# Attention scores, a gate and a planned order: the gate score moved into the matmul of the reads, small work moved to GpSimd, new urgencies for the planner

## The chip, the cores and the metric

The kernel runs on one core of a Trainium2 chip. The metric is device time in microseconds, the median of three runs, and less is better. Five engines take part, each with a queue of its own that it works off in order: TensorE (PE in the profile, PEld for its weight loads), VectorE (DVE), ScalarE (ACT), GpSimd (POOL) and SyncE (SP, which here only issues DMAs). They wait for each other through semaphores.

## The reference

There are 8 batches. In each, 8 heads have 512 rows of x and 32 rows of state, 64 wide. The x rows read the state by softmax, and the state rows read x by softmax. Both results together, 544 rows of 512 (the heads side by side), are the input of a mixture-of-depths block: a gate score per row, the 128 rows with the highest scores of each batch go through two layers, and what comes out is added to them, times the sigmoid of the score.

```python
scores = scale * np.matmul(x, state.transpose(0, 1, 3, 2))
a = np.exp(scores - scores.max(-1, keepdims=True)); a /= a.sum(-1, keepdims=True) + 1e-09
xread = np.matmul(a, state)
...
sread = np.matmul(a2, x)
x = np.concatenate([xread, sread], axis=2)  # then (B, S, H*D)
scores = np.einsum('bsd,d->bs', x, w_gate)
top_idx = np.argpartition(-scores[b], capacity)[:capacity]
ye = np.maximum(x[b, top_idx] @ w1, 0.0) @ w2
out[b, top_idx] = x[b, top_idx] + g[:, None] * ye   # g is the sigmoid of the score
```

All data are float32; x is 8 x 8 x 512 x 64, w1 512 x 1024, w2 1024 x 512.

## The kernel before, in words

The program is cut into pieces (`add`), each a few instructions on one engine with a length in us, the pieces it comes after, the buffers it takes or uses, a key, and for a DMA the time until it has landed. `carry_out` plans all of them ahead of the run: it keeps a clock per engine, finds the engine on which a piece can start first, and among the pieces of that engine that can start within SOON (0.25 us) of it puts down the one with the lowest key. A piece on another engine is seen HOP (0.2 us) after its end. The order so found is the order of the instructions of each engine; on the chip it stays as it is, whatever the real times are. Buffers come from rings: a piece can take one only when all users of the buffer that held the place before it are planned.

One batch goes through these pieces. `attention`: four turns of x on TensorE into ps_tr (L302) with ScalarE copies to xT (L305); scores into ps_s (L325); on VectorE a 32 x 32 transpose into e (turn_in, L339), the maximum (L343), its subtraction (L346), exp on ScalarE (L349), sum and reciprocal (L353 to L355), the product (L358), a transpose into eT (turn_out, L361); for the state side a maximum (s_max, L367), exp on ScalarE (L371), the sums (L376, L377), two turns of a (L418) with copies (L421), the product with x (L434) and its scaling (L439). The reads of the state, `read` (L402), come in two pieces of 16 passes into the one buffer of ps_o, each followed by a ScalarE copy of 1024 columns to xs (L405). SP stores xs (L461) and the state rows (L466).

`choice`: the gate scores, four VectorE products of xs with wg that sum up (gate, L485), for the state rows a product (L491), a sum over heads on TensorE (L498) and a copy (L501). Then the scores are spread along rows (row_x L514, row_s L517, copies L520 and L523), compared with each other (win, L533), counted on TensorE (wins_over, L560) and turned to places (offsets L566, one_hot L573). parts (L544 to L547) splits the scores into three bf16 numbers. pick (L588) finds the chosen rows' numbers and scores, index (L592, L593) makes a row number of them. fetch is GpSimd's gather by row number out of the stored output (L473), which waits for the batch's stores. below (L602 to L604), exps (L607) and sigmoid (L611 to L613) make the gate's weight.

`layers`: it works on the rows of batch 0 alone, then 1 and 2, 3 and 4, 5 and 6, and 7 alone. The rows are turned (L644, copies to xg L647), go through the first layer (L661, relu L665) and the second (L678), VectorE adds (L681) and GpSimd writes the rows back by number (put, also L473). The keys: attention and choice of batch b have (b, n), the layers (100 + number, n), and relu, add and put (-1, number).

Setup: SP loads the first states (L167), x of batch 0 in four pieces (L246), the other states (L170), wg spread over 128 partitions (L174), x of 1 and 2, w1 (L256), x of 3, w2 (L259). GpSimd spreads the states into st_v (pool_states, L202 to L205 and L199) when both loads have landed, and then makes the tables (pool_tables, L211 to L224). row_numbers (L228 to L232) is on VectorE. The states are turned on TensorE (L276, L280). Buffers: ps_tr has two, ps_s and ps_o one of 1024 columns each, ps_h two, xf five (the first of them holds the states until they are spread and turned, and x of batch 4 takes its place).

## Time and profile before

| | us |
|---|---|
| device time, median of 3 runs | 248.92 |
| lowest and highest | 247.83, 250.1 |
| device time of the profiled execution | 248.68 |
| its span, first to last instruction | 246.9 |
| PE, DVE, ACT, POOL busy in it | 209.8, 145.8, 86.0, 32.4 |
| mean granted clock of TensorE | 0.92 of 2.4 GHz |

The profile is that of one execution. The span leaves out what lies ahead of the first instruction and behind the last, so the device time is a little longer. The granted clock of TensorE has two levels: 1.00 is 2.4 GHz, 0.50 is 1.2 GHz, and a number between is a stretch that holds both. A matmul of fp32 weights shows as two instructions.

### The profile page before, as it was taken

To read this page: it belongs to the slowest core of one execution; us is meant where nothing else is said; L and a number is where in the kernel's file an instruction comes from. 1 tells how busy PE (TensorE), PEld (TensorE's weight loads), DVE (VectorE), ACT (ScalarE), POOL (GpSimd) and SP (SyncE) were. 2 spreads that over 40 slices of the span, in tenths; PEclk is the share of its full clock that TensorE was granted. 3 is DMA by queue.
4 is the path that set the end of the run, shared out by engine and by line. 5 is a ranking of instruction groups with operands and counts; after the bars stand their busy time and mean duration, and the time that the engine had idled before them with its cause. 6 is when DMAs were issued, how large, how long until landed. Compare 5 with 4: busy or idle time off the path is not lost.

```text
span 246.9 us, 4781 instructions
## 1 busy us (share of the span) xinstructions
PE 209.8 (85%) x1928; PEld 150.7 (61%) x1928; DVE 145.8 (59%) x430; ACT 86.0 (35%) x159; POOL 32.4 (13%) x60
## 2 busy tenths in 40 slices
PE   2668837959999995774979999999999999999991
PEld 2457524748794663652867877656884478745940
DVE  0375999696899999889899998985000110011001
ACT  3366543644546553255535537111112001200000
POOL 5492000200100021020010001032000110001101
PEclk9977995786999999775999999999999999999998
DMA  6999392269445052050050030630200110001101
GB/s 178 281 379 323 71 357 96 85 234 322 135 136 226 0 190 83 11 212 0 24 206 1 23 150 11 216 98 21 66 0 3 42 42 1 0 0 45 42 0 42
DMA packets 17559, 26.86 MB, mean 109 GB/s; under 512 B 5632, under 2 KB 13824, under 8 KB 16512
## 3 DMA queue, kind: packets, MB, share of 16 engines
q1 hardware_dynamic: 16256, 22.35, 26.9%
q0 software_dynamic: 1280, 4.20, 5.1%
q8 instruction: 15, 0.25, 0.4%
q14 instruction: 8, 0.07, 0.1%
HBM read 15.53 MB, written 11.01 MB: 108 GB/s over the span
## 4 chain that ended last, share of the span: by engine, by line
PE 29%; DVE 28%; issue 28%; ACT 4%; DMA 4%; POOL 3%; SPq 2%; POOLq 1%; DVEq 0%; ACTq 0%
PE ps_o L402 7%; PE ps_h L678 6%; PE ps_h L661 4%; DVE scr L485 4%; DMA xf<-in_x_dram 4%; PE ps_tr L302 3%; DVE win L533 3%; DVE eT L361 3%; DVE e L358 2%; DVE sm L353 2%; DVE e L346 2%; DVE nm L367 2%; PE ps_tr L434 2%; PE ps_tr L418 2%; POOL out_dram L473 2%
## 5 line engine op out<-in xcount | busy, mean ns | idle before, releaser
L661 PE MATMUL ps_h<-xg,w 128*128 128x256 f32 (+1 forms) x320 | 59.5, 345 | 0.7 <-ACT xg L647 0.7
L678 PE MATMUL ps_h<-w,hT 128*128 128x512 f32 x128 | 58.0, 598 | 0.0
L661 PEld LDWEIGHTS ps_h<-xg,w 128*128 128x128 f32 x320 | 52.3, 196 | 7.3 <-issue 1.4
L681 DVE SCALAR_TENSOR_TENSOR ot<-ps_h,z,xr 128x512 f32<-128x512 f32 x8 | 6.0, 750 | 67.2 <-PE ps_h L678 67.2
L678 PEld LDWEIGHTS ps_h<-w,hT 128*128 128x128 f32 x128 | 23.3, 190 | 24.6 <-issue 24.3
L665 ACT ACTIVATE hT<-ps_h 128x512 f32<-128x512 f32 x16 | 9.5, 596 | 61.5 <-PE ps_h L661 61.5
L302 PE MATMUL ps_tr<-ident,xf 128*128 128x128 f32 x128 | 23.8, 344 | 5.6 <-DMA xf<-in_x_dram 4.5
L402 PE MATMUL ps_o<-st_v,eT 64*128 64x128 f32 x256 | 22.2, 323 | 4.6 <-DVE rs L376 4.2
L473 POOL DMA_INDIRECT xr<-out_dram,idx x8 | 8.9, 1112 | 125.2 <-DVE z L602 79.9
L305 ACT COPY xT<-ps_tr 128x512 f32<-128x512 f32 x32 | 18.2, 590 | 18.7 <-PE ps_tr L302 15.5
L405 ACT COPY xs<-ps_o 128x1024 f32<-128x1024 f32 x16 | 16.2, 1014 | 23.1 <-PE ps_o L402 23.1
L302 PEld LDWEIGHTS ps_tr<-ident,xf 128*128 128x128 f32 x128 | 18.3, 176 | 9.5 <-DMA xf<-in_x_dram 2.9
L402 PEld LDWEIGHTS ps_o<-st_v,eT 64*128 64x128 f32 x256 | 18.9, 223 | 7.8 <-DVE rs L376 5.4
L485 DVE SCALAR_TENSOR_TENSOR scr<-xs,wg 128x512 f32<-128x512 f32 x32 | 22.0, 686 | 2.2 <-ACT xs L405 1.3
L325 PE MATMUL ps_s<-xT,st_T 64*32 64x256 f32 x256 | 10.8, 447 | 9.6 <-ACT a L371 9.6
L473 POOL DMA_INDIRECT out_dram<-ot,idx x8 | 8.1, 1018 | 79.9 <-DVE ot L681 64.9
L533 DVE SCALAR_TENSOR_TENSOR win<-srow,sc,after 128x544 bf16<-128x544 f32 (+4 forms) x40 | 18.0, 508 | 0.7 <-ACT srow L523 0.7
L339 DVE STREAM_TRANSPOSE e<-ps_s 128x1024 f32<-128x1024 f32 x8 | 9.9, 1237 | 9.5 <-PE ps_s L325 9.5
L418 PE MATMUL ps_tr<-ident,a 128*128 128x128 f32 x64 | 11.0, 312 | 2.1 <-ACT xT L305 2.1
L325 PEld LDWEIGHTS ps_s<-xT,st_T 64*32 64x32 f32 x256 | 4.4, 120 | 13.7 <-ACT a L371 10.9
L421 ACT COPY aT<-ps_tr 128x512 f32<-128x512 f32 x16 | 9.1, 589 | 7.5 <-PE ps_tr L418 7.5
L349 ACT ACTIVATE e<-e 128x1024 f32<-128x1024 f32 x8 | 8.5, 1061 | 9.1 <-DVE e L346 9.1
(81 smaller groups left out, 221.1 us busy)
## 6 DMA issues: line engine op xcount, KB each, us to landing
out_dram<-xs SPq DMA_DIRECT2D x8, 1024.0 KB, 4.3
xf<-in_x_dram SPq DMA_DIRECT2D x14, 512.0 KB, 7.9
w<-in_moe_w_dram SPq DMA_DIRECT2D x2, 2048.0 KB, 12.8
xf<-in_x_dram SPq DMA_DIRECT2D x4, 256.0 KB, 4.3
out_dram<-xt SPq DMA_DIRECT2D x32, 16.0 KB, 1.8
xf<-in_state_dram SPq DMA_DIRECT2D x1, 448.0 KB, 5.7
wg<-in_moe_w_gate_dram SPq DMA_DIRECT2D x1, 256.0 KB
xf<-in_state_dram SPq DMA_DIRECT2D x2, 64.0 KB, 2.1
```

The lines of the kernel that those rows point to most:

```text
L302: nc.tensor.transpose(v[:, k, r], xf[b].ap[:, 2 * pair + k, 2 * r:2 * r + 2].rearrange("p w d -> p (w d)"), ident)
L305: nc.scalar.copy(out=t.ap, in_=ps.ap.rearrange("p (k r t) -> p k r t", k=2, r=2))
L325: nc.tensor.matmul(view_s()[Ns * q:Ns * (q + 1), w, g], st_T[half, b, g, Ns * q:Ns * (q + 1)], xT[2 * g + q // 2].ap[half, q % 2].rearrang ...
L339: nc.vector.transpose(out=flat(e), in_=s.ap)
L402: nc.tensor.matmul(po[:, i, w, g], eT.ap[half, w, g, r], st_v[half, b, g], start=True, stop=True)
L405: nc.scalar.copy(out=xs.ap[:, 2 * r:2 * r + 2].rearrange("p w (g i m) -> p w g i m", g=2, i=2), in_=o.ap.rearrange("p (i w g m) -> p w g i ...
L418: nc.tensor.transpose(v[:, c], a.ap[:, g, c % 2, 128 * (c // 2):128 * (c // 2 + 1)], ident)
L473: touches(b, nc.gpsimd.indirect_dma_start(**kw), True)
L485: nc.vector.scalar_tensor_tensor(scr, xs.ap[:, c], 1.0, wg, op0=ALU.mult, op1=ALU.mult, accum_out=sc[:, b, c:c + 1])
L533: nc.vector.scalar_tensor_tensor(wins[c].ap[0:n], srow.ap[0:n, f:SP], sc[0:n, b, c:c + 1], after[0:n, 0:SP - f], op0=ALU.is_gt, op1=ALU.mu ...
L661: nc.tensor.matmul(v[:, f, 0:n], w1[:, j, 128 * (f0 + f):128 * (f0 + f + 1)], xg.ap[:, j, 0:n], start=(j == 0), stop=(j == ND - 1))
L678: nc.tensor.matmul(py.ap[0:m], hT.ap[:, f, lo:lo + m], w2[:, f], start=(f == 0), stop=(f == NF - 1))
```

## The change

Scores: st_v gets a 129th column that holds the product of each state row with wg's part for its head, summed. It is made by two new VectorE pieces (state_gates, batch 0 and the rest). The reads come in four pieces of 8 passes and 129 columns; a VectorE reduction of four numbers out of ps_o, two halves and two groups, gives the gate scores of 128 rows (gate). The four products of 512 columns go. ScalarE copies 512 columns four times.

Small work: parts and below run on GpSimd.

Setup: wg is loaded as four DMAs, ahead of the states; the tables come first on GpSimd, the states of batch 0 apart from those of the rest, and batch 0 waits for its own only. Two of the four xT copies of batch 0 are on VectorE. The landing times of loads are longer in the plan.

Planner: HOP is 0.12, SOON one number per engine, and the key of a piece is its batch (or the number of its layers, or the place in the loads) plus a number by its name out of the table LATER. A negative number makes a piece urgent, a positive one puts it behind later batches.

```diff
+    HOP = 0.12
+    SOON = {"PE": 0.06, "DVE": 0.14, "ACT": 0.00, "POOL": 1.06, "SP": 0.30}
+
+    LATER = {
+        "add": -100.00, "below": -1.19, "exp": -5.06, "exps": -28.39, "fetch": -3.70, "first": 100.00,
+        "gate": -18.46, "gate_s": 0.17, "heads": -4.40, "in": 3.76, "index": -27.38, "load": -50.00,
+        "load_x": -2.00, "max": 24.19, "mult": 17.73, "numbers": 33.62, "off": -2.95, "oh": 6.91, "out": -6.90,
+        "over": -7.75, "parts": 7.97, "pick": 4.65, "put": -100.00, "read": 29.38, "relu": -100.00, "row": -6.12,
+        "row_kept": 5.51, "row_s": -5.75, "row_s_kept": -1.26, "rows": -19.12, "score_s": -8.06, "scores": 3.78,
+        "second": 100.00, "sexp": 18.58, "sigmoid": 11.57, "smax": -6.54, "sread": 2.79, "srows": -9.01,
+        "ssum": -3.94, "state_T": 0.63, "state_gates": -11.60, "states": -3.99, "states_0": -0.25, "store": -17.38,
+        "sub": -3.18, "sum": 5.99, "tables": -11.53, "turn": 1.73, "turn_a": -4.60, "turned": -0.03,
+        "turned_a": 4.41, "win": 1.13, "xg": 90.00, "xg_kept": -100.00,
+    }
...
+            self.name, self.key = key[1], key[0] + LATER.get(key[1], 0.0)
...
-            at, p = min(((at, p) for at, p in ready if p.engine == e and at <= t + SOON), key=lambda r: r[1].key)
+            at, p = min(((at, p) for at, p in ready if p.engine == e and at <= t + SOON[e]), key=lambda r: r[1].key)
...
-        nc.sync.dma_start(out=wg, in_=bass.AP(tensor=moe_w_gate.tensor, offset=moe_w_gate.offset,
-                                              ap=[[0, 128], [1, Dm]]))
+        for q in range(4):
+            nc.sync.dma_start(out=wg_s[Ns * q:Ns * (q + 1)],
+                              in_=bass.AP(tensor=moe_w_gate.tensor, offset=moe_w_gate.offset + D * q,
+                                          ap=[[0, Ns], [4 * D, 2], [1, D]]))
...
-    st_v = const.tile([128, B, 2, 2 * D], F32, name="st_v")
+    st_v = const.tile([128, B, 2, 2 * D + 1], F32, name="st_v")
...
-    def pool_states():
+    def pool_states_0():
         nc.gpsimd.memset(st_v[:, 0:1], 0.0)
         state_V(0, 1)
-        nc.gpsimd.memset(st_v[:, 1:B], 0.0)
+
+    def pool_states():
         nc.gpsimd.tensor_copy(out=st_c[:, 1:B, :, 1], in_=st_c[:, 1:B, :, 0])
         state_V(1, B)
 
+    def state_gates(lo, hi):
+        t = work.tile([128, hi - lo, 2, D], F32, name="state_g", tag="hT", bufs=1)
+        nc.vector.tensor_tensor(out=t, in0=st_c[:, lo:hi, :, 0],
+                                in1=wg_s.unsqueeze(1).to_broadcast([128, hi - lo, 2, D]), op=ALU.mult)
+        nc.vector.reduce_sum(out=st_v[:, lo:hi, :, 2 * D], in_=t, axis=AX.X)
...
+        nc.gpsimd.memset(st_v[:, 1:B], 0.0)
...
-    load_x(0, (0, 1), 4)
-    p_st = add("SP", 1.5, load_st, key=(0, 2), lands=1.5, uses=[stb])
-    p_wg = add("SP", 0.8, load_wg, key=(0, 3), lands=1.5)
-    load_x(1, (0, 4))
-    load_x(2, (0, 5))
+    load_x(0, (1, "load"), 4)
+    p_wg = add("SP", 0.4, load_wg, key=(2, "load"), lands=2.5)
+    p_st = add("SP", 1.5, load_st, key=(3, "load"), lands=2.5, uses=[stb])
+    load_x(1, (4, "load"))
+    load_x(2, (5, "load"))
     p_w1 = add("SP", 6.0, lambda: nc.sync.dma_start(out=w1, in_=moe_w1.rearrange("(j p) f -> p j f", p=128)),
-               key=(0, 6), lands=1.5)
-    load_x(3, (0, 7))
+               key=(6, "load"), lands=2.5)
+    load_x(3, (7, "load"))
     p_w2 = add("SP", 6.0, lambda: nc.sync.dma_start(out=w2, in_=moe_w2.rearrange("(j p) m -> p j m", p=128)),
-               key=(0, 8), lands=1.5)
-    p_pool = add("POOL", 8.0, pool_states, after=[p_st0, p_st], key=(0, 0), uses=[stb])
-    p_tab = add("POOL", 6.0, pool_tables, after=[p_wg], key=(0, 1))
-    p_num = add("DVE", 1.0, row_numbers, after=[p_tab], key=(0, 40))
+               key=(8, "load"), lands=2.5)
+    p_tab = add("POOL", 3.8, pool_tables, key=(0, "tables"))
+    p_num = add("DVE", 1.0, row_numbers, after=[p_tab], key=(0, "numbers"))
+    p_pool0 = add("POOL", 1.6, pool_states_0, after=[p_st0], key=(0, "states_0"), uses=[stb])
+    p_pool = add("POOL", 5.6, pool_states, after=[p_st0, p_st, p_tab], key=(0, "states"), uses=[stb])
+    p_sg0 = add("DVE", 0.4, lambda: state_gates(0, 1), after=[p_pool0, p_wg], key=(0, "state_gates"), uses=[stb])
+    p_sg = add("DVE", 2.3, lambda: state_gates(1, B), after=[p_pool, p_wg, p_sg0], key=(1, "state_gates"), uses=[stb])
...
+            on = "DVE" if b == 0 and pair % 2 else "ACT"
...
-        p_xs = []
-        for r in range(2):
+        p_xs, p_sc = [], []
+        for c in range(NC):
             o = Buf(P_O)
 
-            def read(r=r, o=o):
-                po = o.ap.rearrange("p (i w g m) -> p i w g m", i=2, w=2, g=2)
-                for w in range(2):
-                    for g in range(2):
-                        for i in range(2):
-                            half = slice(D * i, D * (i + 1))
-                            nc.tensor.matmul(po[:, i, w, g], eT.ap[half, w, g, r], st_v[half, b, g], start=True, stop=True)
-
-            def keep(r=r, o=o):
-                nc.scalar.copy(out=xs.ap[:, 2 * r:2 * r + 2].rearrange("p w (g i m) -> p w g i m", g=2, i=2),
-                               in_=o.ap.rearrange("p (i w g m) -> p w g i m", i=2, w=2, g=2))
-
-            p = add("PE", 1.16, read, after=[p_eT, p_pool], takes=[o], uses=[eT], key=key(5))
-            p_xs.append(add("ACT", 1.0, keep, after=[p], takes=[] if r else [xs], uses=[o] + ([xs] if r else []), key=key(5)))
+            def view(o):
+                return o.ap.rearrange("p (i g m) -> p i g m", i=2, g=2)
+
+            def read(c=c, o=o):
+                for g in range(2):
+                    for i in range(2):
+                        half = slice(D * i, D * (i + 1))
+                        nc.tensor.matmul(view(o)[:, i, g, 0:2 * D + 1], eT.ap[half, c % 2, g, c // 2], st_v[half, b, g],
+                                         start=True, stop=True)
+
+            def keep(c=c, o=o):
+                nc.scalar.copy(out=xs.ap[:, c].rearrange("p (g i m) -> p g i m", g=2, i=2),
+                               in_=view(o)[:, :, :, 0:2 * D].rearrange("p i g m -> p g i m"))
+
+            def gate(c=c, o=o):
+                nc.vector.tensor_reduce(out=sc[:, b, c:c + 1], in_=view(o)[:, :, :, 2 * D], axis=AX.XY, op=ALU.add)
+
+            p = add("PE", 0.58, read, after=[p_eT, p_pool if b else p_pool0, p_sg if b else p_sg0], takes=[o], uses=[eT],
+                    key=key("read"))
+            p_sc.append(add("DVE", 0.15, gate, after=[p, p_tab], uses=[o], key=key("gate")))
+            p_xs.append(add("ACT", 0.6, keep, after=[p], takes=[] if c else [xs], uses=[o] + ([xs] if c else []), key=key("rows")))
...
-        p_sc = [add("DVE", 0.7, lambda c=c: gate(c), after=[p_xs[c // 2], p_wg, p_tab], uses=[xs], key=key(0))
-                for c in range(NC)]
...
-            nc.vector.tensor_copy(out=s3[:, :, 0], in_=sc[:, b])
-            nc.vector.tensor_tensor(out=rest, in0=sc[:, b], in1=s3[:, :, 0], op=ALU.subtract)
-            nc.vector.tensor_copy(out=s3[:, :, 1], in_=rest)
-            nc.vector.tensor_tensor(out=s3[:, :, 2], in0=rest, in1=s3[:, :, 1], op=ALU.subtract)
-
-        p_3 = add("DVE", 0.7, parts, after=[p_ss, p_num] + p_sc, key=key(3))
+            nc.gpsimd.tensor_copy(out=s3[:, :, 0], in_=sc[:, b])
+            nc.gpsimd.tensor_tensor(out=rest, in0=sc[:, b], in1=s3[:, :, 0], op=ALU.subtract)
+            nc.gpsimd.tensor_copy(out=s3[:, :, 1], in_=rest)
+            nc.gpsimd.tensor_tensor(out=s3[:, :, 2], in0=rest, in1=s3[:, :, 1], op=ALU.subtract)
+
+        p_3 = add("POOL", 0.8, parts, after=[p_ss, p_num] + p_sc, key=key("parts"))
...
-                z = u["z"].ap
-                nc.vector.reduce_sum(out=z[0:m, 2:3], in_=u["ax"].ap[0:m, 2:5], axis=AX.X)
-                nc.vector.tensor_scalar_min(z[0:m, 0:1], z[0:m, 2:3], 0.0)
-                nc.vector.scalar_tensor_tensor(z[0:m, 1:2], z[0:m, 2:3], -1.0, z[0:m, 2:3], op0=ALU.mult, op1=ALU.min)
+                z, ax = u["z"].ap, u["ax"].ap
+                nc.gpsimd.tensor_tensor(out=z[0:m, 2:3], in0=ax[0:m, 2:3], in1=ax[0:m, 3:4], op=ALU.add)
+                nc.gpsimd.tensor_tensor(out=z[0:m, 2:3], in0=z[0:m, 2:3], in1=ax[0:m, 4:5], op=ALU.add)
+                nc.gpsimd.tensor_scalar(z[0:m, 0:1], z[0:m, 2:3], 0.0, None, op0=ALU.min)
+
+                nc.gpsimd.tensor_scalar(z[0:m, 1:2], z[0:m, 0:1], 2.0, None, op0=ALU.mult)
+                nc.gpsimd.tensor_tensor(out=z[0:m, 1:2], in0=z[0:m, 1:2], in1=z[0:m, 2:3], op=ALU.subtract)
...
-            q = add("DVE", 0.45, below, after=[p], takes=[u["z"]], uses=[u["ax"]], key=key(5))
+            q = add("POOL", 0.9, below, after=[p], takes=[u["z"]], uses=[u["ax"]], key=key("below"))
...
-            return (100 + number, n)
-
-        NOW = (-1, number)
+            return (number, n)
...
-            p = add("PE", 0.55, turn, after=[u["got"]], takes=[pt], uses=[u["xr"]], key=key(0))
+            p = add("PE", 0.55, turn, after=[u["got"]], takes=[pt], uses=[u["xr"]], key=key("xg"))
```

## Rows read from the trace of the kernel before

**Rows 1.** Stretches of the span: length, busy per engine, TensorE's clock, DMA share, GB/s.

```profile
0.00:12.00 12.00, 5.88 (x50) 3.88 (x50) 1.65 (x3) 4.21 (x7) 6.15 (x15) 1.00 0.85 225
12.00:24.00 12.00, 9.04 (x92) 7.36 (x96) 8.05 (x10) 7.29 (x14) 7.37 (x14) 0.72 1.03 366
24.00:36.00 12.00, 7.96 (x123) 5.86 (x111) 10.82 (x35) 5.55 (x11) 0.00 (x0) 1.00 0.62 188
36.00:53.04 17.04, 12.18 (x173) 9.16 (x173) 14.72 (x42) 8.91 (x17) 1.78 (x2) 0.70 0.38 143
53.04:60.00 6.96, 5.48 (x34) 5.11 (x34) 5.10 (x15) 3.49 (x7) 0.00 (x0) 0.54 0.91 288
60.00:96.00 36.00, 33.95 (x516) 24.89 (x513) 33.57 (x96) 18.56 (x37) 3.50 (x6) 0.99 0.43 147
96.00:126.00 30.00, 20.21 (x260) 15.68 (x254) 27.13 (x90) 13.21 (x23) 1.82 (x3) 0.77 0.22 82
126.00:174.00 48.00, 47.44 (x440) 33.74 (x440) 40.97 (x139) 17.38 (x35) 6.29 (x12) 1.00 0.23 77
174.00:246.90 72.90, 67.61 (x270) 45.01 (x268) 3.75 (x5) 7.42 (x13) 5.46 (x10) 0.98 0.06 22
sum 246.90, PE 209.75 PEld 150.68 DVE 145.76 ACT 86.03 POOL 32.37; mean PE 23.31 PEld 16.74 DVE 16.20 ACT 9.56 POOL 3.60
```

**Rows 2.** Timeline, batch 0: start, length, engine, line, instruction; idle before, releaser.

```profile
20.50 1.25 DVE L361 STREAM_TRANSPOSE eT<-e 128x1024 f32<-128x1024 f32 x1
...
45.31 1.67 POOL L473 DMA_INDIRECT xr<-out_dram,idx  x1 [25.51 <-DVE z L602]
...
53.04 1.63 PE L661 MATMUL ps_h<-xg,w 128*128 128x128 f32 x8 [0.68 <-ACT xg L647]
```

**Rows 3.** Groups of VectorE instructions: busy us, mean ns of one, idle before, releasers.

```profile
L485 DVE SCALAR_TENSOR_TENSOR scr<-xs,wg 128x512 f32<-128x512 f32 x32 | 22.0, 686 | 2.2 <-ACT xs L405 1.3 <-DVE scr L491 0.2
L346 DVE TENSOR_TENSOR e<-e,mx 128x1024 f32<-128x1024 f32 x8 | 9.9, 1241 | 0.1
L485 DVE DVE_READ_ACCUMULATOR scr<-xs,wg 128x1 f32 x32 | 2.6, 81 | 0.0
L545 DVE TENSOR_TENSOR rest<-sc,aux 128x5 f32<-128x5 f32 x8 | 1.3, 168 | 0.3
L592 DVE COPY pick<-ps_tr 128x5 f32<-128x5 f32 x8 | 1.3, 159 | 2.2 <-PE ps_tr L588 2.2
```

**Rows 4.** Groups of GpSimd instructions.

```profile
L474 POOL MEMSET z<- 128x1 f32 x16 | 1.8, 114 | 0.0
L211 POOL COPY wg_s<-wg 32x128 f32<-32x128 f32 x4 | 1.1, 288 | 0.2
```

**Rows 5.** Waits: engine, line, releaser; total us, times, longest.

```profile
POOL xr L473 <- DMA out_dram<-xt: 26.8, 1, 26.8
```

**Rows 6.** Line L354 (ns: min, median, max), and the timeline around its longest.

```profile
L354 DVE TENSOR_SCALAR sm<-sm x8: 180/182/385, 18.4 to 144.3; 128x32 f32<-128x32 f32 x8
...
17.19 1.59 POOL L215 TENSOR_SCALAR after<-after 128x544 f32<-128x544 f32 x1
18.43 0.39 DVE L354 TENSOR_SCALAR sm<-sm 128x32 f32<-128x32 f32 x1
```

**Rows 7.** Timeline of SP's queue, the first loads.

```profile
0.74 0.97 SPq L167 DMA_DIRECT2D xf<-in_state_dram  x2
...
4.30 2.61 SPq L174 DMA_DIRECT2D wg<-in_moe_w_gate_dram  x1
```

**Rows 8.** Groups of TensorE instructions: the two layers and the reads.

```profile
L661 PE MATMUL ps_h<-xg,w 128*128 128x256 f32 (+1 forms) x320 | 59.5, 345 | 0.7 <-ACT xg L647 0.7
L678 PE MATMUL ps_h<-w,hT 128*128 128x512 f32 x128 | 58.0, 598 | 0.0
L402 PE MATMUL ps_o<-st_v,eT 64*128 64x128 f32 x256 | 22.2, 323 | 4.6 <-DVE rs L376 4.2
```

**Rows 9.** Timeline: the fetch of batch 1's rows, and their turn on TensorE.

```profile
65.28 0.96 POOL L473 DMA_INDIRECT xr<-out_dram,idx  x1 [18.18 <-DMA xf<-in_x_dram]
...
122.98 0.63 PE L644 MATMUL ps_tr<-ident,xr 128*128 128x128 f32 x4
```

More of the change, by code (lines that the diff above doesn't have):

```diff
@@ L84, in __init__ @@
         def __init__(self, engine, length, fn, after, takes, uses, key, lands):
-            self.engine, self.length, self.fn, self.key, self.lands = engine, length, fn, key, lands
-            self.after, self.takes, self.end = [p for p in after if p], takes, None
-            self.uses = uses
-            self.done = None
+            self.engine, self.length, self.fn, self.lands = engine, length, fn, lands
+            self.name, self.key = key[1], key[0] + LATER.get(key[1], 0.0)
+            self.after, self.takes, self.uses = [p for p in after if p], takes, uses
             for buf in list(takes) + list(uses):
@@ L98, in carry_out, with since @@
     def carry_out():
-        free = {}
+        free, taken, done, end, order = {}, {R_X: [stb], stb: True}, {}, {}, []
         left = list(pieces)
-        HOP, SOON = 0.2, 0.25
+        def since(p, q):
+            return end[q] + HOP if q.engine != p.engine else done[q]
         while left:
@@ L121, in carry_out @@
             t, e = min(((at, p.engine) for at, p in ready), key=lambda r: r[0])
-            at, p = min(((at, p) for at, p in ready if p.engine == e and at <= t + SOON), key=lambda r: r[1].key)
+            at, p = min(((at, p) for at, p in ready if p.engine == e and at <= t + SOON[e]), key=lambda r: r[1].key)
+            for buf in p.takes:
+                taken[buf.ring].append(buf)
+                taken[buf] = True
+            free[e] = done[p] = at + p.length
+            end[p] = done[p] + p.lands
+            order.append(p)
+            left.remove(p)
+        for p in order:
             for buf in p.takes:
@@ L125, in carry_out @@
             p.fn()
-            free[e] = p.done = at + p.length
-            p.end = p.done + p.lands
-            left.remove(p)
     def sbuf(name, shape, bufs, dtype=F32, where=None):
@@ L236 @@
     first_exp()
-    p_st0 = add("SP", 0.3, load_st0, key=(0, 0), lands=1.8, uses=[stb])
+    p_st0 = add("SP", 0.3, load_st0, key=(0, "load"), lands=3.2, uses=[stb])
     xf, p_x, last_load = {}, {}, []
@@ L327, in scores @@
                                          start=True, stop=True)
-        p_s = add("PE", 1.09, scores, after=p_xT + [p_sT[b]], takes=[s], uses=xT, key=key(1))
+        p_s = add("PE", 1.09, scores, after=p_xT + [p_sT[b]], takes=[s], uses=xT, key=key("scores"))
         e, eT, a = Buf(R_E), Buf(R_ET), Buf(R_A)
@@ new lines, in attention @@
+        p_exp = add("ACT", 1.06, x_exp, after=[p], uses=[e], key=key("exp"))
+        p_nm = add("DVE", 1.19, s_max, after=[p_s], uses=[s], key=key("smax"))
+        p_a = [add("ACT", 0.8, lambda g=g: s_exp(g), after=[p_nm], takes=[] if g else [a], uses=[s] + ([a] if g else []),
+                   key=key("sexp")) for g in range(2)]
+        p = add("DVE", 1.75, x_sum, after=[p_exp], uses=[e], key=key("sum"))
+        p = add("DVE", 1.23, x_mult, after=[p], uses=[e], key=key("mult"))
+        p_eT = add("DVE", 1.24, turn_out, after=[p], takes=[eT], uses=[e], key=key("out"))
@@ L421, in keep @@
                 nc.scalar.copy(out=t.ap, in_=ps.ap.rearrange("p (c m) -> p c m", c=NC))
-            p = add("PE", 0.53, turn, after=[p_a[g]], takes=[ps, t], uses=[a], key=key(6))
-            p_aT.append(add("ACT", 0.59, keep, after=[p], uses=[ps, t], key=key(6)))
+            p = add("PE", 0.53, turn, after=[p_a[g]], takes=[ps, t], uses=[a], key=key("turn_a"))
+            p_aT.append(add("ACT", 0.59, keep, after=[p], uses=[ps, t], key=key("turned_a")))
             aT.append(t)
@@ L538, in choice @@
             p_w.append(add("DVE", 0.17 + 0.14 * (NC - c), lambda c=c: win(c), after=[p_r1, p_r2] + p_w[-1:],
-                           takes=[wins[c]], uses=[srow], key=key(2)))
+                           takes=[wins[c]], uses=[srow], key=key("win")))
         def parts():
```

126 lines of the change are left out of this document (57 added, 69 removed).

## The prediction

> **What bounds the kernel now.** I read the stretches of the span first (busy time of each engine and TensorE's granted clock, [rows 1]), then the groups of instructions, then single instructions in order of time. The reader is to see two regimes in [rows 1]. From 174 us on TensorE is busy without a gap (67.61 of 72.90 us, the rest being the tail) and VectorE does next to nothing (3.75 us): only the two layers are left. Before 126 us TensorE has gaps and VectorE is nearly full from 24 us on: 33.57 us of 36 in 60 to 96, 27.13 of 30 in 96 to 126. So the attention and the choice of rows run at VectorE's pace, and TensorE fills up with layers what it can get.
>
> TensorE's account, all from [rows 1]: it is busy 209.75 us. What a half clock cost is busy time times (1 - granted clock), where 1.00 is 2.4 GHz and 0.50 is 1.2 GHz: 9.04 x 0.28 = 2.5 (12 to 24 us), 12.18 x 0.30 = 3.7, 5.48 x 0.46 = 2.5, 33.95 x 0.01 = 0.3, 20.21 x 0.23 = 4.6; in all 13.6. So 196 us of work at full clock. The tail behind its last matmul is 72.90 - 67.61 = 5.3 us. The other 246.9 - 196 - 5.3 = 45.6 us are gaps and half clock, and they are all that this change can win, since no matmul goes away.
>
> Where the 45.6 lie: the first layer of batch 0 starts at 53.04 us [rows 2]. Until then TensorE has done 5.9 + 6.5 + 8.0 + 8.5 = 28.9 us of work at full clock, so 24.1 us are lost ahead of it, and 21.5 behind it. Of those behind, 96 to 126 us alone holds 30 - 20.21 + 4.6 = 14.4.
>
> The times are of one execution: span 246.9, device time 248.68, so 1.8 us lie around the span; the median of the runs is 248.92, 0.1% more, and I let that stand as the same.
>
> **The change, part by part.**
>
> *Scores as a 129th column.* It removes the 32 VectorE products of xs with wg: 22.0 us and 32 accumulator reads of 2.6 us [rows 3]. It adds 32 reductions of 4 numbers in PSUM; the nearest row is the copy of 5 numbers from PSUM, 159 ns [rows 3], so 32 x 0.15 to 0.16 = 5 us. I bound one between 0 and the 0.69 of the product that goes: 0 to 22 us, and take 5. TensorE streams 129 columns in place of 128, 1/128 of its reads, some 0.1 us; no row has an odd count of fp32 columns, so the bounds are nothing and, if a read took twice as long, its row again, 22 us [rows 8]. I take the former, as the row of 128 columns is the nearest. The column itself costs two VectorE instructions of 896 elements (1241 ns for 1024 [rows 3], so 1.1 each) and two for batch 0 (0.3 each): 2.8 us, early.
>
> *Small work to GpSimd.* VectorE loses four instructions a batch in parts and three in below, 56 in all; at the 168 ns of the row of one of them that is 9.4 us [rows 3]. GpSimd gets 9 a batch, 72 in all. Bounds for one are the memset of one column, 0.114 us, and the copy of 32 x 128, 0.288 [rows 4]: 8 to 21 us; I take 0.2, 14 us in all. They hide under GpSimd's idle time (busy 32.37 of 246.90 [rows 1]), and parts runs beside row, win, over and one-hot. What is queued behind them is the gather of the rows (fetch); what they themselves queue behind is a fetch that waits for its store, once for 26.8 us [rows 5]. Without that cover, pick of the next batch would wait.
>
> On the port, the trace shows once what happens when both run: the 32-column TENSOR_SCALAR took 385 ns once against a median of 182, at 18.43 us, while GpSimd's 1.59 us instruction (start 17.19) was running until 18.78 [rows 6]. The Trainium skill, "SBUF — State Buffer", section "Who interferes with whom", says that the two engines share a port pair as an exclusive lock and the later one waits for the whole instruction; the trace agrees with that case. By it each of the 72 could hold VectorE for its own 0.2 us at most, 14 us in all, a pace of 15.5 rather than 13.7 us a batch, and the forecast below would be 2 us later.
>
> *Setup.* Tables go ahead of the states on GpSimd, the states of batch 0 apart from the rest; two of batch 0's four xT copies move to VectorE (some 0.65 each, between 0.16 and 0.69, [rows 3]: 1.3 us, and at most 0.6 us of an earlier start). wg's load moves ahead of that of the states on SP's queue as four DMAs; a pair took SP 0.97 us, the one it replaces 2.61 [rows 7], so SP is past it some 0.6 us sooner, and the states' issue comes up to 2 us later, for batch 1 on. I cost that at nothing and keep it inside the uncertainty of the start.
>
> *Four reads in place of two* through the one ps_o buffer: each now waits for the ACT copy and the VectorE reduction of the one ahead. Behind a waiting read on TensorE stand layer pieces of four passes, 4 x 58.0/128 = 1.8 us [rows 8]; behind a waiting reduction on VectorE stands the next batch. I cost both at nothing beyond the chain below; a rival takes the other end.
>
> *VectorE's sum:* 145.76 - 24.6 - 9.4 + 5 + 2.8 + 1.3 = 121. Less the eight additions at the end of the layers (512 columns as the gate's product, some 0.7 to 0.75: 6), row_numbers (five short instructions, some 1.1) and the new setup (4.1), a batch costs (145.8 - 7.1)/8 = 17.3 us before and (121 - 11.2)/8 = 13.7 after.
>
> *First layer.* Before, batch 0's probabilities are turned at 20.50 + 1.25 = 21.75 us, its rows are fetched at 45.31, and the first layer starts at 53.04 [rows 2]. On VectorE, between the first two, batch 0's four gates (4 x 0.77) shrink to 4 x 0.15, parts (0.7) and the numbers (1.1) leave: -4.3. The rest that stands in between is batch 1's softmax, seven and a half passes of 1.24 us [rows 3], 9.3; the consumers of choice (index, off, score_s, row, over) now have negative urgencies, so I let half of it go: -4.6. Between fetch and layer I take 1 us of the 7.7 as waiting that goes. Against that, four reads in a row take 1 us more than two, and the probabilities come some 1 to 3 us later (state_gates of the other batches, 2.2, goes first by its urgency of -11.6): +2. Together 53.0 - 4.3 - 4.6 - 1 + 1 + 2 = 46, and with batch 0's earlier start 45.5; I take 45. Bounds are 40 (all of batch 1's passes go) and 53 (nothing goes).
>
> *Sum.* Work done by 45 us: 28.9 less 8 us at the rate of 24 to 53 us (16.5 us of work in 29, 0.57) is 24.3, plus 1.7 for the faster pace: 26. Left: 196 - 26 = 170. Losses behind it: TensorE should have layers whenever attention leaves it time. The layers are 59.5 + 58.0 = 117.5 us of TensorE [rows 8], so attention needs (196 - 117.5)/8 = 9.8 a batch in 13.7 of VectorE, and a pair of batches brings some 29 us of layers. The two rows in which it is so fed now, 60 to 96 and 126 to 174 us, lose 2.4 and 0.6 of 84 us [rows 1], 3.5%; attention would last until some 140 us, so 95 x 3.5% = 3.3. End of TensorE: 45 + 170 + 3.3 = 218.3; plus 5.3 plus 1.8 is 225.4, with the column and small change **226 us**, 9% faster. A first layer 5 us sooner or 8 later moves it by 0.43 a us, -2.2 to +3.4; losses of 1.2% or 6.6% by -2 to +3. Its own range is 218 to 234.
>
> **Rivals.**
>
> *The dry spell comes back (240 us).* Batch 1's rows were fetched at 65.28 us but turned for the layers only at 122.98 [rows 9]: that turn has the lowest urgency but for the layers, and needs one of two ps_tr buffers, and TensorE ran nearly dry from 96 to 126. The key is 90 now where it was 100, still behind all attention, and ps_tr is still two. For it: the order is written ahead, from lengths. Against: the VectorE pieces that free ps_tr (index, off, score_s) are now urgent. It adds the 14.4 us of that stretch: 240, between 234 and 246.
>
> *In-order stalls at the reductions (slower, 252 us).* The gate reductions have an urgency of -18.46 and VectorE takes its queue in order. If each is reached before TensorE has done the read, because a layer piece of 1.8 us was put ahead, VectorE stands, half a piece on average: 32 x 0.9 = 29 us, more than the 24.8 saved. Forecast and before lie 22.7 us apart for 24.8 us of VectorE, 0.91 each, so this gives 226 + 26 = 252. It decides from 0.78 us a reduction. For it: eight copies of pick out of PSUM waited for TensorE, 2.2 us in all [rows 3]. Against: that is 0.3 each.
>
> *The saved time does not reach TensorE (248 us).* The first layer stays at 53 us and the dry spell stays; VectorE idles instead. Against: VectorE is full in those stretches.
>
> *Faster than thought (215 us).* First layer at 35 us, since none of batch 1 stands in between and state_gates waits, and 1% lost behind: work ahead is 26 - 10 x 0.57 = 20.3, so 35 + 175.7 + 1 + 5.3 + 1.8 = 219; with some layers' turns of x ahead of it (up to 4 us), 215. Against: the reads' chain alone takes most of that time.
>
> **How the numbers follow.** Forecast 0.66, dry spell 0.20, stalls 0.05, no reach 0.04, faster still 0.05. A measurement here can tell about 1% from no change (246.4 to 251.4). Faster: 0.66 + 0.20 + 0.05 = 0.91; same 0.04; slower 0.05. The range from 216 to 243 leaves out the fast case, the two slow ones and a quarter of the dry spell: 0.19.
>
> **What would show it.** VectorE near 121 us and GpSimd near 46; the reductions near 0.15 us and no wait of VectorE on ps_o above 0.5 us each; first layer near 45 us; no stretch after it where TensorE falls under 90% or its clock under 0.95; the last gather of rows near 140 us; TensorE's work still 196. Wrong, if TensorE's reads grow, if xg turns again long after its fetch, or if GpSimd's parts are late for pick.

## The result, and the profile after

The changed kernel takes **223.33 us** (median of 4 runs, 221.41 to 223.9), the one before 248.4 (4 runs, 247.83 to 250.1): a ratio of 0.897, with a 95% interval of 0.889 to 0.904. The forecast was 226.0. The profiled execution has a span of 222.1 us and took 223.9. Here and below a few runs were slower at a lower granted clock (one each of e4, e10 and e13, two of e7's five): they are in the medians and not in the ratios, without them the medians of e4, e7 and e13 are 230.07, 243.66 and 238.91 us, and the profiles of e4 and e7 are of such runs and stay out of the accounts.

The stretches of the span of the changed kernel, cut as in [rows 1] (length, busy time of TensorE, its weight loads, VectorE, ScalarE and GpSimd, TensorE's granted clock, DMA share, GB/s):

```profile
0.00:12.00 12.00, 6.67 (x53) 4.43 (x54) 3.95 (x11) 2.94 (x5) 8.86 (x22) 1.00 0.78 224
12.00:24.00 12.00, 9.20 (x141) 6.95 (x139) 11.76 (x15) 7.71 (x15) 2.58 (x3) 0.86 1.05 380
24.00:36.00 12.00, 10.28 (x172) 7.73 (x172) 10.32 (x29) 10.70 (x25) 0.80 (x4) 1.00 0.66 247
36.00:53.04 17.04, 14.50 (x260) 11.54 (x260) 12.79 (x39) 9.09 (x20) 3.33 (x9) 0.90 0.39 117
53.04:60.00 6.96, 6.57 (x82) 5.75 (x81) 6.79 (x10) 4.86 (x10) 0.49 (x3) 1.00 0.89 263
60.00:96.00 36.00, 34.57 (x538) 25.96 (x538) 32.70 (x100) 23.79 (x53) 8.62 (x22) 1.00 0.39 135
96.00:126.00 30.00, 29.83 (x267) 22.74 (x266) 26.29 (x69) 12.91 (x25) 4.89 (x17) 1.00 0.26 91
126.00:174.00 48.00, 48.00 (x250) 30.60 (x249) 15.65 (x79) 9.37 (x21) 13.71 (x42) 1.00 0.23 83
174.00:222.10 48.10, 42.82 (x182) 28.82 (x180) 3.01 (x4) 4.06 (x7) 4.46 (x8) 0.97 0.06 22
sum 222.10, PE 202.45 PEld 144.52 DVE 123.25 ACT 85.43 POOL 47.73; mean PE 22.49 PEld 16.06 DVE 13.69 ACT 9.49 POOL 5.30
```

Against [rows 1]: the dry stretch from 96 to 126 us is full (29.83 of 30 at a clock of 1.00, where it was 20.21 at 0.77), and from 24 to 53 us TensorE is busy 24.78 us in place of 20.14, at clocks of 1.00 and 0.90 in place of 1.00 and 0.70. VectorE is done with the attention well before 174 us: 15.65 us of 48 in 126 to 174, where it was 40.97.

For the accounts below I split the span as the prediction did, in windows of 2 us: TensorE's work is its busy time times the granted clock; what lies before the first matmul of the first layer and is no work is lost ahead, the rest, less the tail of 5.3 us, lost behind. Before: 195.0 of work, 24.7 ahead, 22.0 behind. After: 199.3, 15.5 and 2.0. So 9.2 and 20.0 us are won, and 4.3 are paid in work.

The timeline of the changed kernel where [rows 2] and [rows 9] stood (start, length, engine, line, instruction; idle time before it): the fetches of batch 0 and 1, their turns, and the first layer.

```profile
40.97 1.91 POOL L513 DMA_INDIRECT xr<-out_dram,idx  x1 [9.70 <-DVE idx L626]
48.41 0.84 PE L679 MATMUL ps_tr<-ident,xr 128*128 128x128 f32 x4
52.61 1.61 PE L696 MATMUL ps_h<-xg,w 128*128 128x128 f32 x13
...
68.20 1.05 POOL L513 DMA_INDIRECT xr<-out_dram,idx  x1 [14.52 <-DVE idx L626]
91.07 0.66 PE L679 MATMUL ps_tr<-ident,xr 128*128 128x128 f32 x4
```

The first layer starts where it did (52.61, before 53.04), though the fetch of its rows starts 4.3 us sooner; between fetch and layer TensorE is given attention to do. Batch 1's rows now wait 23 us for their turn, where they waited 58.

The groups that answer to [rows 3, 4, 8] (busy us, mean ns of one, idle time before):

```profile
L696 PE MATMUL ps_h<-xg,w 128*128 128x256 f32 (+1 forms) x320 | 59.2, 340 | 0.0
L713 PE MATMUL ps_h<-w,hT 128*128 128x512 f32 x128 | 58.6, 599 | 0.0
L436 PE MATMUL ps_o<-st_v,eT 64*128 64x129 f32 x256 | 23.4, 302 | 0.9 <-ACT xs L440 0.7
...
L444 DVE TENSOR_REDUCE sc<-ps_o 128x1 f32<-128x4 f32 x32 | 5.0, 156 | 9.5 <-PE ps_o L436 4.6 <-ACT xs L440 4.4
...
L635 POOL TENSOR_TENSOR z<-pick 128x1 f32<-128x1 f32 x8 | 2.7, 336 | 0.0
L577 POOL CAST aux<-sc 128x5 bf16<-128x5 f32 x8 | 2.5, 316 | 38.8 <-DVE sc L444 23.2
L640 POOL TENSOR_TENSOR z<-z 128x1 f32<-128x1 f32 x8 | 1.6, 194 | 0.7
```

The 32 products of 22.0 us and their accumulator reads of 2.6 have become 32 reductions of 5.0.

### The profile page after: what moved, and what is told of

It is laid out like the page before. It is cut to its first block, busy times and chain, and to the rows that moved or that the text cites. A ratio compares the mean times of both kernels' runs of the same rounds, so it can differ in the third digit from the quotient of the medians.

```text
span 222.1 us, 4789 instructions
## 1 busy us (share of the span) xinstructions
PE 202.4 (91%) x1928; PEld 144.5 (65%) x1928; DVE 123.2 (55%) x348; ACT 85.4 (38%) x173; POOL 47.7 (21%) x128
## 4 chain that ended last, share of the span: by engine, by line
PE 44%; issue 21%; DVE 12%; DMA 6%; POOL 6%; ACT 6%; SPq 3%; POOLq 1%
PE ps_h L713 12%; PE ps_h L696 11%; PE ps_o L436 7%; DMA xf<-in_x_dram 3%; DMA xr<-out_dram,idx 3%; PE ps_tr L329 3%; PE ps_tr L474 2%; DVE win L566 2%; POOL out_dram L513 2%; POOL xr L513 2%; PE ps_tr L679 2%; DVE sm L386 2%; PE ps_tr L458 2%; DVE nm L400 1%; PE ps_tr L593 1%
## 5 line engine op out<-in xcount | busy, mean ns | idle before, releaser
L696 PEld LDWEIGHTS ps_h<-xg,w 128*128 128x128 f32 x320 | 50.8, 191 | 6.6 <-issue 1.4
L329 PE MATMUL ps_tr<-ident,xf 128*128 128x128 f32 x128 | 20.8, 308 | 7.5 <-DMA xf<-in_x_dram 6.6
L566 DVE SCALAR_TENSOR_TENSOR win<-srow,sc,after 128x544 bf16<-128x544 f32 (+4 forms) x40 | 18.4, 509 | 15.5 <-ACT srow L556 15.5
L440 ACT COPY xs<-ps_o 128x512 f32<-128x512 f32 x32 | 18.7, 586 | 15.9 <-DVE sc L444 10.1
L436 PE MATMUL ps_o<-st_v,eT 64*128 64x129 f32 x256 | 23.4, 302 | 0.9 <-ACT xs L440 0.7
L329 PEld LDWEIGHTS ps_tr<-ident,xf 128*128 128x128 f32 x128 | 16.1, 157 | 10.9 <-issue 4.9
L436 PEld LDWEIGHTS ps_o<-st_v,eT 64*128 64x128 f32 x256 | 17.2, 190 | 5.2 <-ACT xs L440 2.2
L404 ACT ACTIVATE a<-ps_s,nm 128x512 f32<-128x512 f32 x16 | 11.1, 700 | 1.2 <-DVE e L372 0.6
L577 POOL CAST aux<-sc 128x5 bf16<-128x5 f32 x8 | 2.5, 316 | 38.8 <-DVE sc L444 23.2
L474 PE MATMUL ps_tr<-xf,aT 128*32 128x64 f32 x512 | 9.7, 232 | 0.8 <-ACT aT L461 0.5
L386 DVE TENSOR_REDUCE sm<-e 128x32 f32<-128x1024 f32 x8 | 9.6, 1201 | 1.2 <-ACT e L382 1.2
## 6 DMA issues: line engine op xcount, KB each, us to landing
w<-in_moe_w_dram SPq DMA_DIRECT2D x2, 2048.0 KB, 14.5
```

The lines of the kernel that those rows point to most:

```text
L329: nc.tensor.transpose(v[:, k, r], xf[b].ap[:, 2 * pair + k, 2 * r:2 * r + 2].rearrange("p w d -> p (w d)"), ident)
L386: nc.vector.reduce_sum(out=sm, in_=e.ap, axis=AX.X)
L404: nc.scalar.activation(out=a.ap[:, g], in_=view_s()[:, :, g], func=AF.Exp, bias=tmp["nm"][:, g:g + 1], accum_out=tmp["ss"][:, g:g + 1])
L436: nc.tensor.matmul(view(o)[:, i, g, 0:2 * D + 1], eT.ap[half, c % 2, g, c // 2], st_v[half, b, g], start=True, stop=True)
L440: nc.scalar.copy(out=xs.ap[:, c].rearrange("p (g i m) -> p g i m", g=2, i=2), in_=view(o)[:, :, :, 0:2 * D].rearrange("p i g m -> p g i m"))
L474: nc.tensor.matmul(o2.ap[rr, D * g:D * (g + 1)], aT[g].ap[:, c, rr], xf[b].ap[:, 4 * g + q, c], start=(c == 0), stop=(c == NC - 1))
```

## The experiments

Two theories stood against each other. By the one, which takes the figure of the forecast's stalls rival for a rule, VectorE's time is what is won: 0.91 us of time for each us of VectorE. By the other, the order that the planner writes down is what counts, and VectorE's load only moves that order. Each kernel was timed beside the kernel before on the same chip (its median was 251.04 us beside e1 to e4, 249.66 beside e7 to e10, 249.25 beside e11 to e14); ratios are to those. No kernel leaves work out; two add VectorE products that nothing reads.

**e1: the scores as VectorE products again.** Reads of 128 columns, in four pieces; everything else as after.

```diff
-                nc.vector.tensor_reduce(out=sc[:, b, c:c + 1], in_=view(o)[:, :, :, 2 * D], axis=AX.XY, op=ALU.add)
...
+                nc.vector.scalar_tensor_tensor(scr, xs.ap[:, c], 1.0, wg, op0=ALU.mult, op1=ALU.mult,
+                                               accum_out=sc[:, b, c:c + 1])
```

> The gate scores are products of xs with wg on VectorE again (32 of 0.69 us), the reads have 128 columns; urgencies, setup and GpSimd's small work stay as after the change. Theory V (VectorE's load sets the pace, so TensorE runs dry): VectorE is 123 + 17 = 140 us busy, time 223 + 0.91 x 17 = 238 us (234 to 243), and TensorE falls under 90% in some stretch between 60 and 126 us. Theory O (the new order alone keeps TensorE fed): 224 to 229 us, no such stretch.

Measured: 239.13 us, 0.954 [0.946, 0.963]; VectorE 138.2. That is the time of the first theory, but the planner wrote another order here too, and the loss lies ahead of the first layer, which starts at 89.48 us (account below). The reads in its groups of TensorE instructions:

```profile
L436 PE MATMUL ps_o<-st_v,eT 64*128 64x128 f32 x256 | 23.4, 302 | 5.0 <-DVE eT L394 3.6 <-ACT xs L440 1.4
```

The busy time and the mean are those of the reads of 129 columns: the added column costs nothing that shows.

**e2: e1, and the small work back on VectorE too.** What is left of the change is the four reads, the setup and the planner's part.

```diff
-            nc.gpsimd.tensor_copy(out=s3[:, :, 0], in_=sc[:, b])
...
+            nc.vector.tensor_copy(out=s3[:, :, 0], in_=sc[:, b])
...
-        p_3 = add("POOL", 0.8, parts, after=[p_ss, p_num] + p_sc, key=key("parts"))
+        p_3 = add("DVE", 0.7, parts, after=[p_ss, p_num] + p_sc, key=key("parts"))
```

> As the run with the products back, and parts and below are on VectorE too: what is left of the change is the setup and the new urgencies. Theory V: VectorE near 149 us, time 223 + 0.91 x 26 = 246 us (241 to 250), close to before. Theory O: 225 to 232 us, most of the gain stays.

Measured: 252.83 us, 1.010 [1.000, 1.020]. With VectorE's load as before (145.7 us), the new planner alone gains nothing; it is slower than either theory had it (246 us, and 225 to 232).

**e3: everything but the planner.** Old urgencies and allowances.

```diff
-    HOP = 0.12
...
+    HOP = 0.2
...
-            self.name, self.key = key[1], key[0] + LATER.get(key[1], 0.0)
+            self.name, self.key = key[1], old_key(key[0], key[1])
```

> Everything of the change but its planner: the keys of before, HOP 0.2 and SOON 0.25. Theory V: VectorE stays at 123 us, so most of the gain stays: 224 to 232 us. Theory O: the dry stretch comes back, 238 to 248 us, with a stretch of 20 us or more behind the first layer in which TensorE is under 80% busy.

Measured: 241.25 us, 0.961 [0.953, 0.970], with VectorE at 125.0. That is the time of the second theory, though TensorE is busier in its poorest stretch than that theory said (24.45 us of the 30 from 96 to 126, or 82%). VectorE's 20.8 us less win about 10 here, half of what 0.91 would give.

**e4: the small work alone back on VectorE** (the second edit of e2, on the changed kernel).

> As after, but parts and below on VectorE again. Theory V: 9 us more on VectorE, 223 + 8 = 231 us (228 to 234). Theory O: 222 to 226 us, since VectorE had room left.

Measured: 230.4 us, 0.916 [0.907, 0.925]. The first theory had 231; but this kernel too was planned anew, so how much of the 7 us is the load and how much the order is not told apart.

**e7: the old setup, planned anew.** GpSimd lays out all states ahead of the tables, wg is loaded behind the states, ScalarE copies every xT.

```diff
-    p_tab = add("POOL", 3.8, pool_tables, key=(0, "tables"))
+    p_pool0 = add("POOL", 1.6, pool_states_0, after=[p_st0], key=(-20, "tables"), uses=[stb])
+    p_pool = p_pool0 = add("POOL", 7.2, pool_states, after=[p_st0, p_st, p_pool0], key=(-10, "tables"), uses=[stb])
+    p_tab = add("POOL", 2.2, pool_tables, after=[p_pool], key=(0, "tables"))
```

> After the change, but with the setup of before: the load of the states ahead of wg's, the states of all batches spread before the tables and before the first read, all four xT copies of batch 0 on ScalarE. Theory V (VectorE's work sets the time): VectorE starts some 1 us later and waits for the states' gates, 224 to 227 us where before takes 248.4 (ratio 0.90 to 0.915). Theory S (the order fits only the very pieces and lengths it was chosen with): any change of the pieces costs, 228 to 238 us.

Measured: 244.28 us, 0.977 [0.968, 0.987]. That seemed to make the setup worth 21 us; but the planner had written another order from the first pieces on: the first layer starts at 105.44 us in the profiled execution. e12 tells the two apart.

**e8: the urgencies rounded to whole numbers.**

```diff
-        "gate": -18.46, "gate_s": 0.17, "heads": -4.40, "in": 3.76, "index": -27.38, "load": -50.00,
...
+        "gate": -18.0, "gate_s": 0.0, "heads": -4.0, "in": 4.0, "index": -27.0, "load": -50.0,
```

> After the change with every number of LATER rounded to a whole one; no instruction is added, removed or made longer, only the order of some may change. Theory V: 222 to 225 us where before takes 248.4 (ratio 0.893 to 0.907), for VectorE's work is the same. Theory S: 227 to 238 us (ratio above 0.915), with TensorE losing 5 us or more behind its first layer.

Measured: 223.48 us, 0.894 [0.888, 0.901]. The planned order differs in places, and the time does not: the second digits are worth nothing.

**e9 and e10: VectorE work that the planner does not see,** behind each reduction, so that the order stays that of after; 512 columns in e9, 64 in e10.

```diff
+                scr = small.tile([128, 512], F32, name="scr_x", bufs=1)
+                nc.vector.tensor_tensor(out=scr, in0=idle_a, in1=idle_a, op=ALU.mult)
```

> After the change in its own order, with one VectorE product of 512 columns behind each gate reduction that nothing reads and the plan does not see: some 32 x 0.69 = 22 us of VectorE. Theory V: 0.91 us each, 223 + 20 = 243 us where before takes 248.4 (ratio 0.965 to 0.99). Rival: VectorE has room now and TensorE alone is the bound, 223 to 230 us (ratio below 0.925).

> The same with a product of 64 columns, some 32 x 0.22 = 7 us of VectorE that the plan does not see. Theory V: 223 + 6 = 229 us (ratio 0.915 to 0.93). Rival (VectorE has room): 222 to 225 us (ratio below 0.907).

Measured: e9 231.3 us, 0.926 [0.919, 0.934]; e10 222.37, 0.890 [0.881, 0.898]. The added products in the groups of VectorE instructions of e9:

```profile
L448 DVE TENSOR_TENSOR scr_x<-idle_a 128x512 f32<-128x512 f32 x32 | 21.7, 677 | 0.0
```

The same in the groups of e10:

```profile
L448 DVE TENSOR_TENSOR scr_x<-idle_a 128x64 f32<-128x64 f32 x32 | 6.9, 215 | 0.0
```

Instructions in a row overlap in the records, so VectorE's busy time rises by less: to 140.4 us in e9 and 127.2 in e10. 6.9 us of instructions cost nothing that can be measured, as the rival had it; 21.7 cost 8.0, or 0.47 a us of added busy time (17.2), between the 20 of the one expectation and the at most 7 of the other.

**e11: the work of before in the order of after.** The planner still sees the pieces of the changed kernel; what they issue is that of before (products of the kept rows, each behind its copy; small work on VectorE).

```diff
+        for p in [p for p in order if p.name == "gate"]:
+            if order.index(p) < order.index(p.behind):
+                order.remove(p)
+                order.insert(order.index(p.behind) + 1, p)
...
+            p_sc[-1].behind = p_xs[-1]
```

> The plan stays that of the changed kernel, piece for piece, with its order on TensorE; only what the pieces issue is put back: the reads take 128 columns, the scores are VectorE products of the kept rows again (each behind its copy), and the small score work runs on VectorE at its planned places. VectorE's busy time should come back to about 145 us. If the planned order carries the gain, the time is 228 to 236 us, as with the unseen products of 22 us (231.3), less or more by what the products' wait for the copies costs. If VectorE's load carries it by 0.91 us for each us, the time is near 223 + 0.91 x 22 = 243 us or above.

Measured: 238.1 us, 0.955 [0.950, 0.960], VectorE 143.9: between the two expectations. Two of its stretches behind the first layer:

```profile
96.00:126.00 30.00, 27.73 (x346) 20.66 (x345) 28.68 (x94) 13.44 (x27) 3.96 (x6) 1.00 0.28 103
126.00:150.00 24.00, 22.53 (x142) 14.58 (x142) 21.83 (x73) 8.65 (x17) 1.99 (x3) 1.00 0.26 99
```

The products in its groups of VectorE instructions:

```profile
L451 DVE SCALAR_TENSOR_TENSOR scr_g<-xs,wg 128x512 f32<-128x512 f32 x32 | 21.7, 679 | 6.5 <-ACT xs L446 6.5
```

VectorE is nearly full until 150 us (28.68 us of 30, 21.83 of 24) and TensorE has small gaps all along; of the 14.5 us between its span and that of after, 2.8 lie ahead of the first layer, 9.6 behind it, and 2.1 are work. Beyond e9, the products also stand still for ScalarE's copies (6.5 us); how much of the 6.8 us between e9 and e11 that wait is, is not told apart.

**e12: the setup of before in the order of after.** The setup's pieces are moved after the planning; the large zeroing and the copies of xT are as in e7.

```diff
+        later = order[order.index(p_sg) - 1]
+        for p, q in ((p_wg, p_st), (p_pool0, p_st), (p_pool, p_pool0), (p_tab, p_pool), (p_num, later), (p_sg0, p_num)):
+            move(p, q)
```

> The plan is that of the changed kernel; afterwards only the setup's pieces are moved to where they stood in the kernel before: the gate weights load behind the states, GpSimd lays out the states (with the large zeroing) ahead of the tables, the three pieces of VectorE that need these stand later, and the first batch's turned tiles are all copied by ScalarE. If the 244.28 us of the earlier run with the old setup came from the other order that the planner then chose for everything behind it, the time is at most 230 us. If the setup itself is what costs, by a late start of the reads, it is 238 us or more.

Measured: 223.16 us, 0.897 [0.892, 0.902]. The first read starts 0.3 us later than in the changed kernel (24.24, 23.94), and that is worth nothing; the some 20 us of e7 were the order. Three things of the new setup stay in e12: wg's four loads, the planned landing times, and that the plan lets batch 0 wait for its own states alone.

**e13: only the allowances of before.**

```diff
-    HOP = 0.12
-    SOON = {"PE": 0.06, "DVE": 0.14, "ACT": 0.00, "POOL": 1.06, "SP": 0.30}
+    HOP = 0.2
+    SOON = {"PE": 0.25, "DVE": 0.25, "ACT": 0.25, "POOL": 0.25, "SP": 0.25}
```

> Everything as in the changed kernel but the planner's two allowances, which are those of before: 0.2 us for a hop between engines, and 0.25 us within which a more urgent piece may be waited for, alike on every engine. If the urgencies carry what the planner's part of the change gives, the time stays within 223 to 228 us; if the allowances matter as much, it lies nearer to the 241.25 us of the run in which urgencies and allowances were both those of before.

Measured: 239.51 us, 0.961 [0.954, 0.968], as slow as e3, with the new urgencies and with VectorE at 123.9. Its timeline, with the fetches of batch 0's and 1's rows, their turn and the first layer:

```profile
51.19 1.33 POOL L513 DMA_INDIRECT xr<-out_dram,idx  x1 [2.71 <-DVE idx L626]
57.11 1.93 POOL L513 DMA_INDIRECT xr<-out_dram,idx  x1 [3.14 <-DVE scr L526]
...
86.38 1.09 PE L679 MATMUL ps_tr<-ident,xr 128*128 128x128 f32 x8
...
88.54 1.06 PE L696 MATMUL ps_h<-xg,w 128*128 128x128 f32 x8
```

Three of its stretches:

```profile
60.00:72.00 12.00, 8.29 (x92) 5.82 (x89) 10.16 (x20) 10.24 (x21) 1.19 (x6) 0.95 0.37 139
72.00:96.00 24.00, 23.25 (x336) 18.55 (x334) 20.18 (x53) 12.10 (x24) 3.98 (x11) 0.74 0.18 62
96.00:126.00 30.00, 29.86 (x291) 21.86 (x289) 27.53 (x78) 14.47 (x30) 4.29 (x13) 1.00 0.20 80
```

The fetches of two batches' rows start by 57.11 us, and a fetch lands in 3.6 us here (the median), yet the first layer runs at 88.54. From 60 to 72 us TensorE does 8.29 us of 12, most of it with that work lying ready, and in 72 to 96 its clock is 0.74. TensorE takes its instructions in the written order, and in this one attention stands ahead of the layers until then.

**e14: the fetched rows turned at once.**

```diff
-        "turned_a": 4.41, "win": 1.13, "xg": 90.00, "xg_kept": -100.00,
+        "turned_a": 4.41, "win": 1.13, "xg": -50.00, "xg_kept": -100.00,
```

> Everything as in the changed kernel, but the turning of the fetched rows is made urgent (90 becomes -50), so that the first layer can begin as soon as the rows are there. If what counts is that the first layer starts early, as the forecast had it, the first layer comes at about 45 us and the time falls by up to 7 us, to about 216. If what counts is that TensorE always has something to run, whichever work it is, the time stays within 2% of 223 us, or is longer where attention work is then missing later.

Measured: 223.27 us, 0.896 [0.891, 0.901]. The turn and the first layer in its timeline:

```profile
47.62 0.66 PE L679 MATMUL ps_tr<-ident,xr 128*128 128x128 f32 x4
...
51.84 0.83 PE L696 MATMUL ps_h<-xg,w 128*128 128x128 f32 x6
```

The first layer hardly moved, so a layer at 45 us was not tried; batch 1's rows are turned at 71.83 us in place of 91.07, for nothing.

The account of each profiled execution, worked out as above (us; the parts and the tail of 5.3 make the span):

```
kernel                        VectorE  work   first layer  ahead  behind  median
before                        145.8    195.0     53.04     24.7   22.0    248.4
after                         123.2    199.3     52.61     15.5    2.0    223.33
e10 (+6.9 unseen)             127.2    199.3     50.97     13.9    2.1    222.37
e12 (old setup, same order)   121.3    199.3     51.76     14.7    2.0    223.16
e14 (turned at once)          124.3    199.8     51.84     14.8    2.4    223.27
e8  (rounded urgencies)       123.8    199.8     51.71     15.1    2.9    223.48
e9  (+21.7 unseen)            140.4    200.3     53.22     16.1    7.8    231.3
e11 (old work, same order)    143.9    201.4     54.79     18.3   11.6    238.1
e13 (old allowances)          123.9    201.5     88.54     27.3    3.0    239.51
e3  (old planner)             125.0    199.1     57.61     22.3   12.7    241.25
e1  (products, planned anew)  138.2    200.8     89.48     28.9    1.4    239.13
e2  (old work, planned anew)  145.7    199.7     94.33     35.7    9.1    252.83
```

Two things are shown. In one order (after, e10, e9, e11) the time rises with VectorE's load, from nothing to 14.8 us, mostly behind the first layer, where VectorE hands TensorE its attention. At one load (after, e13, e3: 123 to 125 us) the order alone makes 16 to 18 us. Against the 25 us won, each half alone wins some two fifths: old work in the new order some 11 (249.25 to 238.1), new work in the old planner's order some 10 (251.04 to 241.25); together they win a little more than the sum.

## Why the prediction was right

**Right in its main account.** VectorE came to 123.2 us (forecast 121), GpSimd to 47.7 (46), a reduction to 156 ns (0.15 us). The dry spell went: lost behind 2.0 us, forecast 3.3. The tail is 48.10 - 42.82 = 5.3 us, and 1.8 lie around the span, both as used. The setup cost nothing, as I put it (e12). In-order stalls at the reductions stayed small: VectorE stood idle 9.5 us before them, 0.3 a reduction, where that rival needed 0.78. The sign that no such wait is above 0.5 us did not hold: the longest were 0.9 us for TensorE and 1.1 for ScalarE's copy, and 4.4 of the 9.5 us are waits for that copy, which I had not seen as one that VectorE waits for. Of the signs of being wrong two showed: TensorE's reads grew, at a cost told below, and batch 1's rows were turned 23 us after their fetch, though no dry spell came of it.

**Right in the sum, wrong in three of its terms.** The first layer was to start at 45 us; it started at 52.61. The step that failed is the one that read, from negative urgencies, that half of batch 1's passes and 1 us of the wait between fetch and layer would go: that wait grew from 7.7 to 11.6 us, filled with attention. Nor did the passes go: between batch 0's probabilities and its fetch stand eight passes of 1.2 us, as many as before (five of batch 1 and three of later ones, before seven and one), and that stretch fell from 23.6 to 17.7 us where 15.7 was forecast. Of the 7.6 us by which the first layer was missed, 4.9 lie in the wait and 2.1 in the stretch. The next step, work done by then at the old rate of 0.57, failed the other way: by 52.61 us TensorE had done 37.1 us, before 28.3 by 53.04. So 15.5 us are lost ahead, where 45 - 26 = 19 were forecast. Third, TensorE's work was to stay at 196 and came to 199.3: I had costed four reads in place of two at nothing. One of sixteen passes took 1.16 us, and the next work began 1.09 us after it; one of eight takes 0.72, and the next begins 0.65 after. The timelines of before and after, both at a clock of 1.00 there:

```profile
25.43 1.16 PE L402 MATMUL ps_o<-st_v,eT 64*128 64x128 f32 x16
26.52 1.09 PE L302 MATMUL ps_tr<-ident,xf 128*128 128x128 f32 x8
...
23.94 0.72 PE L436 MATMUL ps_o<-st_v,eT 64*128 64x129 f32 x8
24.59 1.09 PE L329 MATMUL ps_tr<-ident,xf 128*128 128x128 f32 x8
```

Two pieces for one cost 2 x 0.65 - 1.09 = 0.21 us, some 3.4 over the 16 pieces of before. Every order with four reads has 199.1 to 201.5 of work, at 128 columns too (e1); the split by itself was not run, and the results also lie further apart in ps_o (256 columns for 128). The errors are -3.5, -1.3 and, against my 196, +3.3 us; that they nearly cancel is luck, and the span is 222.1 for 223.6.

**The last gather** was to come near 140 us and came at 169.93; the seventh is at 140.99. It stood behind a write-back of rows on GpSimd's queue, and nothing hung on it: TensorE was busy 48.00 us of the 48 before 174.

**The rate of 0.91 a us of VectorE,** with which the stalls rival was priced, is refuted as a rule: in the order of after it is about nothing for the first 4 us of busy time, 0.47 over 17.2 (e9) and 14.8 / 20.7 = 0.72 over the whole load (e11). What an order will do can't be read from single urgencies, as that step did: with the same urgencies and other allowances, or with the same allowances and another setup, the planner writes orders that are 16 to 21 us slower (e13, e7). The dry-spell rival's 240 us is what e13, e3 and e1 took (239.1 to 241.3): such an order was near at hand, though in e13 and e1 the loss lies ahead of the first layer and not behind it.

**Open.** Whether the new urgencies find a good order for the pieces of before as they were was not tried; e2, which differs from those only in the four reads and the setup, took 252.83 us. And why this order is good can be told (TensorE nearly always has something), not which urgency makes it so.

## What to carry to other kernels

In a kernel whose order is written ahead by a planner, a change of load and a change of order can't be priced apart: test the load in a fixed order (unseen work, or other work behind the same pieces), and the order at a fixed load. Account for the bound engine as work, loss ahead of the first filler work, and loss behind it: the time is their sum, and when the filler starts matters only through what the engine lacks until then. If an undo of one small part costs far more than its work, look first whether the planner wrote another order.
